# Retention scores in 64x64 array tiles, issued a tile ahead in one piece with the state product

## The chip, the core and the metric

The kernel runs on one core of a Trainium2 chip. The metric is the device time of one execution in microseconds (us), here the median of several executions. All five engines of the core (TensorE, called PE in the profile, with its weight loads PEld; VectorE, DVE; ScalarE, ACT; GpSimd, POOL; SyncE, SP) run their own instruction streams and meet at semaphores.

## The reference, cut to what matters

Three layers follow each other: a retention layer (a recurrent state with a decay for each head), a two-layer MLP with a layer norm, and a mixture of four attention experts of which two are chosen for each token. The change touches the first, and one matrix product of the third.

```python
# q, k, v: (B, H, S, D) = (2, 8, 768, 64)
for t in range(S):                                  # retention
    state = gamma * state + outer(k[t], v[t])
    y[t] = scale * q[t] @ state
x = y as (B, S, 512)
xn = layer_norm(x) * g_ln
x = x + relu(xn @ w_ch1) @ w_ch2                    # 512 -> 2048 -> 512
for e in range(4):                                  # attention experts, head dim 64
    a = softmax(causal(q_e @ k_e.T / 8))
    out += gate_e * (a @ v_e) @ wo[e]
```

## The kernel before

**Retention.** The sequence is cut into chunks of 128 tokens; with two batches that makes 12 tiles, which run in the order (chunk 0, batch 0), (chunk 0, batch 1), (chunk 1, batch 0) and so on. Each tile holds all 8 heads as 4 pairs. For each tile two arrays are loaded by DMA, `kq` (k and q with the head dimension on the partitions, 512 KB, four buffers) and `vk` (v and k with the tokens on the partitions, 512 KB, three buffers), and for each chunk a table `tabY` of 256 KB. `r_tile(i)` then plans:

- POOL scales v by the decay (`vs`, L425).
- `scores` on PE (L435): k transposed times q for each head. The contraction runs over the 64 dimensions of a head, so the two heads of a pair lie in the two row halves of the array (64 rows by 128 columns); 8 products, each of which the trace shows as 2 MATMULs with a weight load of its own.
- DVE multiplies the scores by the causal mask (`am`, L441, two of them).
- `inter` (L454, not for chunk 0): the state of the chunk before times q, in 64 by 64 array tiles, into two PSUM banks `y`.
- `intra` (L463): scaled values times masked scores, added into `y`, in array tiles of 128 rows by 64 columns.
- `upd` (L470, not for the last chunk): the state update, in 128 by 64 tiles too; ACT copies the state out (`sn`, L475), which the `inter` of the same batch's next chunk reads.
- DVE multiplies `y` by `tabY` into `xT` (L479), PE transposes it (L486, full array), DVE, POOL and ACT make the layer norm, PE transposes back (L486 again), ACT and POOL split the result into a high and a low part (`x`) for the MLP.

**PSUM.** It has 8 banks. The state takes one; scores, `y`, both transposes, the scratch of the weight splits and the MLP's sums share the other seven, taken and given back bank by bank.

**The planner.** Nothing is issued in the order of the program text. Every step becomes a `Node` with an engine, a cost in us, what it reads and writes, the buffers it takes, and a priority (`prio`, the order of planning, shifted by `P.bias`). `Plan.issue` plays the kernel through with these costs: whenever an engine is free, it takes the waiting step with the lowest priority number whose inputs are ready and whose buffers fit, all of them at once. The order found is the order in which each engine's instructions are written, DMAs included: they all go out through SP, one queue, and an SP instruction that waits for its buffer holds up those behind it.

**MLP and attention.** The MLP's weights are split into high and low parts as they come (L523 to L548), its products are L592, L611 and L672; for some weight blocks it uses sums of tokens (`x_sums`, POOL, L634 to L641). MLP steps of the first tokens are planned into the retention stage where PE would be idle. In attention `a_turn` (L905) transposes the probabilities and `a_value` (L924) multiplies them by the values, two experts side by side in array tiles of 128 by 64; L948 is the output projection.

Of the kernel before, what the change touches and what calls it, by code (L numbers as in the profile page):

```python
# [28 lines left out]
OP = mybir.AluOpType  # L29
# [7 lines left out]
C = 128  # L37
# [8 lines left out]
NPC = 4  # L46
LATE = 150
ALONE = 4
SEVEN = (2, 3, 4, 5, 6, 7)
NEG = -1000000000.0  # L50
LIMIT = float(np.array(0x0FEFFFFF, np.uint32).view(np.float32))
# [21 lines left out]


class Node:
    __slots__ = ("eng", "fn", "deps", "bufs", "prio", "lat", "end", "left", "succ", "ready")


class Plan:
# [5 lines left out]
        self.readers = {}  # L85
        self.bias = 0

    def add(self, eng, fn, r=(), w=(), lat=0.12, hold=()):
        n = Node()
        n.eng = eng  # L90
# [24 lines left out]
        self.nodes.append(n)  # L115

    def issue(self):
# [29 lines left out]
                    waiting[e].append(n)  # L147
        todo = len(self.nodes)
        order = []
        t = 0.0  # L150
        while todo:
            moved = True
            while moved:
                moved = False
                for e in free:
                    if free[e] > t:
                        continue
                    for n in sorted(waiting[e], key=lambda n: n.prio):
                        if n.ready > t:
                            continue  # L160
                        got = []
# [51 lines left out]
def retention_channel_mlp_mixture_attention(ctx: ExitStack, tc: tile.TileContext, a):  # L213
# [101 lines left out]
    def new(n):  # L315
        return Buf(PL[n], n)

    def PE(c, fn, r=(), w=(), hold=()):
        P.add({"T": c}, lambda e: fn(), r, w, lat=0.2, hold=hold)

    def ACT(c, fn, r=(), w=()):
        P.add({"A": c}, lambda e: fn(), r, w)
# [1 line left out]
    def DVE(c, fn, r=(), w=()):  # L324
        P.add({"V": c}, lambda e: fn(), r, w)
# [4 lines left out]
    def DMA(nbytes, fn, r=(), w=()):  # L330
        P.add({"D": nbytes / 320e3 + 0.05}, lambda e: fn(), r, w, lat=2.2)
# [27 lines left out]

    tiles = [(b, c) for c in range(NC) for b in range(B)]  # L360
    NTI = len(tiles)
    L = {}
    TY = {}

    def r4(ap):
        return ap.rearrange("p (a t) -> p a t", a=4)

    def load(i):
        b, c = tiles[i]
        kq, vk = new("kq"), new("vk")  # L370
        n = 2 if i == 0 else 1
        for y in range(n):
            h = slice(1024 // n * y, 1024 // n * (y + 1))
            DMA(512e3 / n, lambda h=h: sp.dma_start(f32(kq)[:, h], a["kq"][b, c][:, h]), w=[(kq, y)])
            if i == 0 and y == 0:
                DMA(24e3, lambda: sp.dma_start(tabV, a["tabV"]), w=["tabV"])
                DMA(64e3, lambda: sp.dma_start(caus, a["caus"]), w=["caus"])
        for y in range(n):
# [5 lines left out]
        L[i] = (kq, vk)  # L384

    DVE(0.2, lambda: dve.memset(negs, NEG), w=["negs"])
    IDLE = new("ps")
# [13 lines left out]
    DVE(0.1, lambda: dve.memset(half, -0.5), w=["half"])  # L401

# [11 lines left out]

    SN = {}

    def r_tile(i):
        b, c = tiles[i]
        j, cc = divmod(c, TPB)
        kq, vk = L[i]  # L420
        pair = lambda z, p: f32(kq)[:, p // 2 * 512 + z * 256 + p % 2 * C:p // 2 * 512 + z * 256 + (p % 2 + 1) * C]
# [6 lines left out]
        PA, AM = [new("ps") for _ in range(2)], [new("am") for _ in range(2)]  # L428
        ny = 2 if i == 0 else 1
        for y0 in range(ny):  # L430
            def scores(y0=y0):
                for p in range(4 // ny * y0, 4 // ny * (y0 + 1)):
                    for h in range(2):
                        hs = slice(64 * h, 64 * h + 64)
                        pe.matmul(f32(PA[h])[:, p * C:(p + 1) * C], lhsT=pair(0, p)[hs], rhs=pair(1, p)[hs],  # L435
                                  start=True, stop=True)
            PE(1.3 / ny, scores, r=[(kq, y0)] + (["spun"] if i == 0 else []), w=PA + (["scored"] if i == 0 else []), hold=AM)
            if i == 0 and y0:
                spin(2, 0.6, ["scored"], ["spun"])
        for h in range(2):  # L440
            DVE(0.69, lambda h=h: dve.tensor_tensor(r4(f32(AM[h])), r4(f32(PA[h])),  # L441
                                                    caus[:, None, :].to_broadcast([128, 4, C]), OP.mult),
                r=[PA[h], "caus"], w=[AM[h]])
# [3 lines left out]
        if c:  # L447
            def inter():
                for z in range(2):
                    for g in range(2):  # L450
                        for w in range(2):
                            p = 2 * z + g
                            ws = slice(64 * w, 64 * w + 64)
                            pe.matmul(place(g, w, z), lhsT=f32(st)[ws, p * D:(p + 1) * D], rhs=pair(1, p)[ws],  # L454
                                      start=(z == 0), stop=False, skip_group_check=True)
            PE(0.5, inter, r=[st, (kq, 0)], w=y)

        def intra():
            for w in range(2):
                for z in range(2):  # L460
                    for g in range(2):
                        p = 2 * z + g
                        pe.matmul(place(g, w, z), lhsT=h3(f32(vs))[:, 2 * p + w], rhs=r4(f32(AM[w]))[:, p],  # L463
                                  start=(c == 0 and z == 0), stop=True, skip_group_check=True)
        PE(1.0, intra, r=[vs] + AM + (y if c else []) + (["spun"] if i == 0 else []), w=y)
        if c < NC - 1:
            def upd():
                for p in range(NP):
                    for h in range(2):
                        pe.matmul(state(b)[64 * h:64 * h + 64, p * D:(p + 1) * D], lhsT=h3(k())[:, 2 * p + h],  # L470
                                  rhs=h3(f32(vs))[:, 2 * p + h], start=(i == 0 and p == 0), stop=False,
                                  skip_group_check=True)
# [438 lines left out]
    def a_value(b, g, p, PT, last, also=()):  # L911
        nj = 2 * g + 2
        avs, at = [new("psa") for _ in range(2 if last else 1)], new("at")
        for av, zs in zip(avs, ((0,), (1,)) if last else ((0, 1),)):
            for j0 in range(0, nj, 2):
                def mm(j0=j0, zs=zs, av=av):
                    for j in (j0, j0 + 1):
# [4 lines left out]
                        for x in range(2):  # L922
# [44 lines left out]

    pieces = [(f, i) for f in range(NFC) for i in ((2, 3, 0, 1) if f in SEVEN else range(NPC))]
    early = {0: (0, 1), 3: (2, 3), 7: (4, 5), 9: (6, 7)}
    for i in range(NTI):  # L970
        if i + 3 < NTI:
            load(i + 3)
        for n in early.get(i, ()):
            load_piece(*pieces[n])
        r_tile(i)
        for n in early.get(i, ()):
            P.bias += 40
            split_piece(*pieces[n])
            P.bias -= 40
# [129 lines left out]
```

## Time and profile before

| | |
|---|---|
| runs shown | 453.09, 452.96, 452.55 us; median 452.96 us |
| profiled execution, first to last instruction (span) | 450.3 us; no other time is recorded for it |
| PE busy | 439.8 us, 98% of the span |
| DVE, ACT, POOL busy | 328.0, 223.4, 209.4 us |
| granted TensorE clock | 1.000 over the span |
| retention on PE | 3.39 us to 67.9 us, from 39.4 us on with MLP steps among it |
| MLP, then attention | up to about 315 us, then to the end |

Busy times are from the profiled execution. A matmul's end is modelled and matmuls overlap, so the cost of a run of matmuls is best read as the distance from its start to the start of the next run on PE. [...]

### The profile page before, as it was taken

What the parts mean: (1) busy time and instruction counts of PE and PEld (TensorE: products, weight loads), DVE (VectorE), ACT (ScalarE), POOL (GpSimd) and SP (SyncE); (2) the same over time, 40 slices, a digit from 0 to 9 for tenths busy, and PEclk for the clock granted to TensorE, in tenths of its full rate; (3) what the DMA queues carried; (4) which work ended last, traced back from release to release, by engine and by line L of the source; (5) the groups of instructions that cost most, each with busy time, mean ns of one, the idle gap of its engine ahead of it and who ended that gap; (6) DMA issues with size and microseconds to landing.
All of it is one profiled execution on the core that took longest, in us unless ns stands there. A gap on an engine that the chain in (4) does not pass through costs nothing.

```text
span 450.3 us, 8468 instructions
## 1 busy us (share of the span) xinstructions
PE 439.8 (98%) x3198; PEld 415.5 (92%) x3198; DVE 328.0 (73%) x709; ACT 223.4 (50%) x467; POOL 209.4 (47%) x216
## 2 busy tenths in 40 slices
PE   8999999999999999999999999999999999998996
PEld 7778889999999999999999999999999987897875
DVE  2798786868659767877868565569657988878962
ACT  1476566263256335344354164245534756645852
POOL 1688768978989325226155064100401333224440
PEclk9999999999999999999999999999999999999999
DMA  7998923203103104114021002003230220101111
GB/s 263 366 347 325 314 81 108 95 24 118 47 1 140 48 1 134 55 48 140 1 89 53 1 1 93 2 0 95 70 72 20 66 71 33 49 1 47 49 49 47
DMA packets 15129, 40.11 MB, mean 89 GB/s; under 512 B 2288, under 2 KB 4976, under 8 KB 15088
## 3 DMA queue, kind: packets, MB, share of 16 engines
q1 hardware_dynamic: 15088, 39.57, 26.0%
q8 instruction: 25, 0.41, 0.4%
q14 instruction: 16, 0.13, 0.1%
HBM read 33.27 MB, written 3.15 MB: 81 GB/s over the span
## 4 chain that ended last, share of the span: by engine, by line
PE 86%; DVE 5%; DMA 3%; issue 2%; ACT 1%; POOL 1%; SPq 1%; DVEq 0%; ACTq 0%; POOLq 0%
PE ps L611 29%; PE ps L672 19%; PE ps L592 8%; PE ps L756 6%; PE ps L924 4%; PE ps L793 4%; PE ps L905 4%; PE ps L948 3%; DMA vk<-in_vk_dram 3%; PE ps L486 2%; PE ps L863 2%; PE ps L864 2%; PE ps L463 2%; PE ps L435 1%; DVE sm L871 1%
## 5 line engine op out<-in xcount | busy, mean ns | idle before, releaser
L611 PE MATMUL ps<-h,w 128*128 128x384 f32 x768 | 145.6, 335 | 0.7 <-DVE xT L615 0.4
L611 PEld LDWEIGHTS ps<-h,w 128*128 128x128 f32 x768 | 134.0, 188 | 1.4 <-DVE xT L615 0.7
L615 DVE TENSOR_TENSOR xT<-xT,ps 128x384 f32<-128x384 f32 x112 | 60.1, 549 | 36.9 <-PE ps L611 36.6
L885 POOL TENSOR_SCALAR pr<-pr,sm,gate 128x384 f32<-128x384 f32 (+5 forms) x48 | 34.9, 738 | 80.4 <-DVE ps L870 32.8
L548 POOL TENSOR_TENSOR w<-wy,w 128x512 fp32r<-128x512 f32 x26 | 33.7, 1301 | 44.2 <-PE ps L611 39.7
L672 PE MATMUL ps<-t,S 128*128 128x384 f32 x216 | 43.1, 334 | 0.0
L873 ACT ACTIVATE pr<-ps,sm 128x384 f32<-128x384 f32 (+5 forms) x48 | 30.3, 636 | 20.8 <-DVE sm L871 15.5
L679 ACT ACTIVATE u<-ps 128x384 f32<-128x384 f32 x36 | 17.6, 490 | 41.4 <-PE ps L672 35.7
L672 PEld LDWEIGHTS ps<-t,S 128*128 128x128 f32 x216 | 37.9, 188 | 0.1
L592 PE MATMUL ps<-x,w 128*128 128x384 f32 x192 | 34.8, 336 | 0.4 <-ACT wx L523 0.4
L523 ACT ACTIVATE wx<-raw 128x512 f32<-128x512 f32 x32 | 21.5, 672 | 27.5 <-DVE ps L527 19.7
L592 PEld LDWEIGHTS ps<-x,w 128*128 128x128 f32 x192 | 33.2, 188 | 0.8 <-ACT wx L523 0.6
L871 DVE TENSOR_REDUCE sm<-ps 128x1 f32<-128x384 f32 (+5 forms) x48 | 30.0, 624 | 2.9
L524 POOL TENSOR_SCALAR wx<-wx 128x512 f32<-128x512 f32 x32 | 20.3, 633 | 18.5 <-ACT wx L523 17.7
L687 ACT ACTIVATE h<-ps 128x384 fp32r<-128x384 f32 x36 | 17.6, 490 | 22.6 <-PE ps L611 14.4
L672 PE MATMUL ps<-x,w 128*128 128x384 f32 x144 | 28.8, 334 | 0.0
L672 PEld LDWEIGHTS ps<-x,w 128*128 128x128 f32 x144 | 25.3, 188 | 0.0
L905 PE MATMUL ps<-ident,pr 128*128 128x128 f32 x168 | 22.5, 275 | 2.0 <-DVE at L935 1.2
L547 ACT ACTIVATE w<-wy 128x512 fp32r<-128x512 f32 x26 | 16.3, 627 | 16.4 <-PE ps L611 16.1
L525 DVE TENSOR_SCALAR ps<-wx 128x512 uint32<-128x512 uint32 x32 | 22.0, 686 | 2.2 <-POOL wx L524 1.8
L529 DVE SCALAR_TENSOR_TENSOR wy<-raw,ps 128x512 uint32<-128x512 uint32 x32 | 21.8, 682 | 1.9 <-POOL w L548 1.3
L527 DVE SCALAR_TENSOR_TENSOR ps<-wx,ps 128x512 uint32<-128x512 uint32 x32 | 22.3, 696 | 1.1
(123 smaller groups left out, 877.3 us busy)
## 6 DMA issues: line engine op xcount, KB each, us to landing
raw<-in_w_dram SPq DMA_DIRECT2D x32, 512.0 KB, 3.5
kq<-in_kq_dram SPq DMA_DIRECT2D x11, 512.0 KB, 5.5
vk<-in_vk_dram SPq DMA_DIRECT2D x11, 512.0 KB, 5.1
qk<-qk SPq DMA_DIRECT2D x32, 96.0 KB, 2.1
out_dram<-ob SPq DMA_DIRECT2D x11, 256.0 KB, 2.0
tabY<-in_tabY_dram SPq DMA_DIRECT2D x6, 256.0 KB, 5.2
vraw<-in_wv_dram SPq DMA_DIRECT2D x1, 520.0 KB, 3.6
kq<-in_kq_dram SPq DMA_DIRECT2D x2, 256.0 KB, 2.9
```

The lines of the kernel that those rows point to most:

```text
L525: DVE(0.62, lambda: dve.tensor_scalar(u32(z), u32(x), 4, 1, op0=OP.logical_shift_left, op1=OP.logical_shift_right), r=[x], w=[z])
L527: DVE(0.7, lambda: dve.scalar_tensor_tensor(u32(z), u32(x), 0x80000000, u32(z), op0=OP.bitwise_and, op1=OP.bitwise_or), r=[x, z], w=[z])
L548: POOL(1.34, lambda: pool.tensor_tensor(f32r(l), f32(y), f32(h), OP.subtract), r=[y, h], w=[l])
L592: pe.matmul(f32(pa, TB), lhsT=wt, rhs=blk(f32r(xt[b][j]))[:, k], start=(n == 0), stop=(n == 11))
L611: pe.matmul(f32(pa, TB), lhsT=wt, rhs=t, start=(n == 0), stop=(n == 5))
L615: DVE(0.55, lambda: dve.tensor_tensor(blk(f32(xt))[:, k], blk(f32(xt))[:, k], f32(pa, TB), OP.add), r=[pa] + [(xt, cc, w) for cc in range( ...
L672: pe.matmul(f32(pa, TB), lhsT=wt, rhs=t, start=(first and n == 0), stop=(n == 5), skip_group_check=True)
L756: pe.matmul(f32(pa, TB), lhsT=mw(n, lo, k, p * 128, (p + 1) * 128), rhs=blk(f32r(xt))[:, k], start=(i == 0), stop=(i == 11))
L871: dve.tensor_reduce(f32(sm)[:, z:z + 1], halves(f32(s), 512), axis=mybir.AxisListType.XY, op=OP.max, negate=True)
L873: ACT(act_c(nk) + .18, lambda s=s, pr=pr, z=z: act.activation(halves(f32(pr), wide), halves(f32(s), 512), AF.Exp, bias=f32(sm)[:, z:z + 1] ...
L885: POOL(0.28 + nk * 0.95e-3, lambda pr=pr, z=z, e=e: pool.tensor_scalar(f32(pr, nk), f32(pr, nk), f32(sm)[:, 6 + z:7 + z], GT[b, j][:, cc, ...
L905: pe.transpose(f32(pa)[:, i * C:(i + 1) * C], f32(PRS[z][x])[:, j * C:(j + 1) * C], ident)
```

## The change

Four things are edited; the computation stays the same.

1. The scores of tile i+1 are planned inside `r_tile(i)`, and in one PE step with the state product `inter` of tile i (`quarters`). Each 128-column weight block of the scores is cut in two, so that they run in 64 by 64 array tiles: 16 products for each tile instead of 8. The first tile's scores stand alone (`r_first`). The step takes the two `y` banks and the two score banks (`PAS`) together, and holds the two mask buffers (`AMS`).
2. `upd` and `intra` become one PE step (`columns`), the update first, except in the first tile and in the last chunk.
3. `load` is cut into `load_kq` and `load_vk`, and `kq` is planned one tile further ahead than `vk`.
4. Each PE step has a form (whole, quarters, columns). In the planner a step of another form than the last one is sorted 25 places later (`STAY`), and costs 0.16 us more (`SWITCH`). `a_value` is of the form columns, and its planned cost falls from 0.97 and 0.76 to 0.85 and 0.64.

```diff
+STAY = 25
+SWITCH = 0.16
...
-                    for n in sorted(waiting[e], key=lambda n: n.prio):
+                    for n in sorted(waiting[e], key=lambda n: n.prio + STAY * (e == "T" and n.form != form)):
...
                             cost = n.eng[e]
+                            if e == "T":
+                                cost += SWITCH * (n.form != form)
+                                form = n.form
...
-    load(0)
+    load_kq(0)
+    load_vk(0)
     DMA(64e3, lambda: sp.dma_start(ident, a["ident"]), w=["ident"])
-    load(1)
-    load(2)
+    load_kq(1)
+    load_vk(1)
+    load_kq(2)
+    load_kq(3)
+    load_vk(2)
...
+    def scores(i, ps):
+        for p in ps:
+            for m in range(2):
+                for h in range(2):
+                    hs, ms = slice(64 * h, 64 * h + 64), slice(64 * m, 64 * m + 64)
+                    pe.matmul(f32(PAS[i][h])[ms, p * C:(p + 1) * C], lhsT=pair(i, 0, p)[hs, ms], rhs=pair(i, 1, p)[hs],
+                              start=True, stop=True)
+
+    def masked(i):
+        for h in range(2):
+            DVE(0.69, lambda h=h: dve.tensor_tensor(r4(f32(AMS[i][h])), r4(f32(PAS[i][h])),
+                                                    caus[:, None, :].to_broadcast([128, 4, C]), OP.mult),
+                r=[PAS[i][h], "caus"], w=[AMS[i][h]])
...
-            PE(1.3 / ny, scores, r=[(kq, y0)] + (["spun"] if i == 0 else []), w=PA + (["scored"] if i == 0 else []), hold=AM)
...
-            PE(0.5, inter, r=[st, (kq, 0)], w=y)
...
+        if c or i + 1 < NTI:
+            def quarters():
+                if c:
+                    inter()
+                if i + 1 < NTI:
+                    scores(i + 1, range(4))
+            r, w, hold = [], [], []
+            if c:
+                r, w = [st, (KQ[i], 0)], list(y)
+            if i + 1 < NTI:
+                r, w, hold = r + [(KQ[i + 1], 0)], w + PAS[i + 1], AMS[i + 1]
+            PE(0.45 * bool(c) + 0.9 * (i + 1 < NTI), quarters, r=r, w=w, hold=hold, form="quarters")
+        if i + 1 < NTI:
+            masked(i + 1)
...
-        PE(1.0, intra, r=[vs] + AM + (y if c else []) + (["spun"] if i == 0 else []), w=y)
...
+        if c == NC - 1:
+            PE(0.86, intra, r=r1, w=w1, form="columns")
+        elif i == 0:
+            PE(0.86, intra, r=r1, w=w1, form="columns")
+            PE(0.45, upd, r=r2, w=w2, form="columns")
+        else:
+            def columns():
+                upd()
+                intra()
+            PE(1.31, columns, r=r1 + r2, w=w1 + w2, form="columns")
...
-            PE(0.65, upd, r=[(vk, 1), vs] + (["first"] if i == 1 else []), w=[(STATE, b)] + (["first"] if i == 0 else []))
...
-                PE((0.97 if j0 + 2 < nj else 0.76) * len(zs) / 2, mm,
+                PE((0.85 if j0 + 2 < nj else 0.64) * len(zs) / 2, mm, form="columns",
...
+    r_first()
     for i in range(NTI):
+        if i + 4 < NTI:
+            load_kq(i + 4)
         if i + 3 < NTI:
-            load(i + 3)
+            load_vk(i + 3)
```

## Rows read from the trace of the kernel before

**Rows 1.** The page: busy time of PE and DVE, busy tenths of PE and DMA.

```profile
PE 439.8 (98%) x3198; PEld 415.5 (92%) x3198; DVE 328.0 (73%) x709; ACT 223.4 (50%) x467; POOL 209.4 (47%) x216
...
PE   8999999999999999999999999999999999998996
...
DMA  7998923203103104114021002003230220101111
```

**Rows 2.** Windows: stretch, its length, busy us (count) by engine, clock, DMA share, GB/s.

```profile
12.50:20.00 7.50, 7.50 (x123) 6.27 (x124) 5.20 (x14) 2.78 (x5) 4.20 (x6) 1.00 0.96 359
20.00:26.80 6.80, 6.12 (x96) 4.77 (x94) 6.63 (x14) 6.11 (x11) 5.07 (x9) 1.00 0.94 342
...
32.00:38.00 6.00, 5.87 (x105) 5.09 (x105) 4.17 (x10) 4.33 (x8) 5.46 (x8) 1.00 0.98 370
```

**Rows 3.** Timeline of POOL: the value scaling of two tiles.

```profile
18.90 1.04 POOL L425 TENSOR_TENSOR vs<-vk,tabV 128x512 f32<-128x512 f32 x1 [0.39 <-DMA vk<-in_vk_dram]
...
25.74 1.04 POOL L425 TENSOR_TENSOR vs<-vk,tabV 128x512 f32<-128x512 f32 x1
```

**Rows 4.** Timeline of PE in retention: start us, us, engine, line, operation.

```profile
26.84 1.09 PE L463 MATMUL ps<-am,vs 128*64 128x128 f32 x16 [0.60 <-POOL vs L425]
27.76 0.64 PE L470 MATMUL ps<-vs,vk 128*64 128x64 f32 x16
28.32 1.16 PE L435 MATMUL ps<-kq 64*128 64x128 f32 x16
29.49 0.67 PE L454 MATMUL ps<-kq,sn 64*64 64x128 f32 x16
30.09 0.66 PE L486 MATMUL ps<-ident,xT 128*128 128x128 f32 x4
...
33.35 0.63 PE L470 MATMUL ps<-vs,vk 128*64 128x64 f32 x16
33.92 0.67 PE L454 MATMUL ps<-kq,sn 64*64 64x128 f32 x16
34.52 0.66 PE L486 MATMUL ps<-ident,xn 128*128 128x128 f32 x4
...
46.26 0.69 PE L470 MATMUL ps<-vs,vk 128*64 128x64 f32 x16
46.87 1.16 PE L435 MATMUL ps<-kq 64*128 64x128 f32 x16
47.97 1.09 PE L463 MATMUL ps<-am,vs 128*64 128x128 f32 x16
48.99 0.66 PE L486 MATMUL ps<-ident,xn 128*128 128x128 f32 x4
```

**Rows 5.** Timeline of PE: the first MLP step in retention.

```profile
39.37 2.32 PE L592 MATMUL ps<-x,w 128*128 128x384 f32 x12 [0.38 <-ACT wx L523]
```

**Rows 6.** Timeline of weight loads and DVE, 26 to 34 us.

```profile
29.01 0.76 DVE L479 TENSOR_TENSOR xT<-ps,tabY 128x256 f32<-128x256 f32 x2
29.49 0.43 PEld L454 LDWEIGHTS ps<-kq,sn 64*64 64x64 f32 x16 [0.20 <-DVE xT L479]
...
30.09 0.42 PEld L486 LDWEIGHTS ps<-ident,xT 128*128 128x128 f32 x4 [0.17 <-issue]
```

**Rows 7.** Groups by line on PE: busy us, mean ns | idle before.

```profile
L435 PE MATMUL ps<-kq 64*128 64x128 f32 x192 | 15.2, 299 | 1.1 <-DMA kq<-in_kq_dram 1.0
...
L454 PE MATMUL ps<-kq,sn 64*64 64x128 f32 x160 | 6.8, 282 | 0.0
```

**Rows 8.** Waits of SP's queue, 0 to 70 us: total, times, longest.

```profile
SPq L374 <- PE ps L454: 13.7, 6, 3.5
```

**Rows 9.** Timeline of PE: one run of attention's value products.

```profile
425.88 3.25 PE L924 MATMUL ps<-ptn,vv 128*64 128x256 f32 x32
```

**Rows 10.** Timeline of POOL: the last token sums of the MLP.

```profile
142.59 3.65 POOL L641 TENSOR_TENSOR t<-t,t 128x768 fp32r<-128x768 f32 x2
```

**Rows 11.** Timeline of PE: a product that reads token sums.

```profile
146.52 1.20 PE L672 MATMUL ps<-t,S 128*128 128x384 f32 x6
```

More of the change, by code (lines that the diff above doesn't have):

```diff
@@ L75 @@
 class Node:
-    __slots__ = ("eng", "fn", "deps", "bufs", "prio", "lat", "end", "left", "succ", "ready")
+    __slots__ = ("eng", "fn", "deps", "bufs", "prio", "lat", "end", "left", "succ", "ready", "form")
 class Plan:
@@ L86, in __init__, with add @@
         self.bias = 0
-    def add(self, eng, fn, r=(), w=(), lat=0.12, hold=()):
+    def add(self, eng, fn, r=(), w=(), lat=0.12, hold=(), form="whole"):
         n = Node()
+        n.form = form
         n.eng = eng
@@ L149, in issue @@
         order = []
+        form = "whole"
         t = 0.0
@@ L316, in new, with PE @@
         return Buf(PL[n], n)
-    def PE(c, fn, r=(), w=(), hold=()):
-        P.add({"T": c}, lambda e: fn(), r, w, lat=0.2, hold=hold)
+    def PE(c, fn, r=(), w=(), hold=(), form="whole"):
+        P.add({"T": c}, lambda e: fn(), r, w, lat=0.2, hold=hold, form=form)
     def ACT(c, fn, r=(), w=()):
@@ L361, in retention_channel_mlp_mixture_attention, with load_kq @@
     NTI = len(tiles)
-    L = {}
-    TY = {}
+    KQ, VK, TY, PAS, AMS = {}, {}, {}, {}, {}
     def r4(ap):
         return ap.rearrange("p (a t) -> p a t", a=4)
-    def load(i):
+    def load_kq(i):
         b, c = tiles[i]
-        kq, vk = new("kq"), new("vk")
+        kq = new("kq")
         n = 2 if i == 0 else 1
@@ L377, in load, with load_vk @@
                 DMA(64e3, lambda: sp.dma_start(caus, a["caus"]), w=["caus"])
+        KQ[i] = kq
+    def load_vk(i):
+        b, c = tiles[i]
+        vk = new("vk")
+        n = 2 if i == 0 else 1
         for y in range(n):
@@ L383, in load @@
             DMA(256e3, lambda: sp.dma_start(f32(ty), a["tabY"][c]), w=[ty])
-        L[i] = (kq, vk)
+        VK[i] = vk
     DVE(0.2, lambda: dve.memset(negs, NEG), w=["negs"])
@@ L415, in retention_channel_mlp_mixture_attention, with pair, r_first @@
     SN = {}
+    def pair(i, z, p):
+        return f32(KQ[i])[:, p // 2 * 512 + z * 256 + p % 2 * C:p // 2 * 512 + z * 256 + (p % 2 + 1) * C]
+    def scores(i, ps):
[10 more added lines that the diff above has]
+                r=[PAS[i][h], "caus"], w=[AMS[i][h]])
+    def r_first():
+        PAS[0], AMS[0] = [new("ps") for _ in range(2)], [new("am") for _ in range(2)]
+        for y0 in range(2):
+            PE(0.45, lambda y0=y0: scores(0, range(2 * y0, 2 * y0 + 2)), r=[(KQ[0], y0), "spun"], w=PAS[0] + ["scored"], hold=AMS[0],
+               form="quarters")
+        spin(2, 0.6, ["scored"], ["spun"])
+        masked(0)
     def r_tile(i):
@@ L419, in r_tile @@
         j, cc = divmod(c, TPB)
-        kq, vk = L[i]
-        pair = lambda z, p: f32(kq)[:, p // 2 * 512 + z * 256 + p % 2 * C:p // 2 * 512 + z * 256 + (p % 2 + 1) * C]
+        vk = VK[i]
         v, k = lambda: f32(vk)[:, :512], lambda: f32(vk)[:, 512:]
@@ L427, in r_tile @@
              r=[(vk, 0), "tabV"], w=[vs])
[L428 to L436, printed above, removed]
-            PE(1.3 / ny, scores, r=[(kq, y0)] + (["spun"] if i == 0 else []), w=PA + (["scored"] if i == 0 else []), hold=AM)
[L438 to L443, printed above, removed]
         st = SN.get(b)
@@ L446, in r_tile, with inter @@
         place = lambda g, w, z: f32(y[w])[64 * g:64 * g + 64, z * C:(z + 1) * C]
[L447 to L455, printed above, removed]
-            PE(0.5, inter, r=[st, (kq, 0)], w=y)
+        def inter():
+            for z in range(2):
+                for g in range(2):
+                    for w in range(2):
+                        p = 2 * z + g
+                        ws = slice(64 * w, 64 * w + 64)
+                        pe.matmul(place(g, w, z), lhsT=f32(st)[ws, p * D:(p + 1) * D], rhs=pair(i, 1, p)[ws],
+                                  start=(z == 0), stop=False, skip_group_check=True)
+        if i + 1 < NTI:
+            PAS[i + 1], AMS[i + 1] = [new("ps") for _ in range(2)], [new("am") for _ in range(2)]
+        if c or i + 1 < NTI:
[10 more added lines that the diff above has]
+            PE(0.45 * bool(c) + 0.9 * (i + 1 < NTI), quarters, r=r, w=w, hold=hold, form="quarters")
+        if i + 1 < NTI:
+            masked(i + 1)
         def intra():
@@ L462, in intra, with upd @@
                         p = 2 * z + g
-                        pe.matmul(place(g, w, z), lhsT=h3(f32(vs))[:, 2 * p + w], rhs=r4(f32(AM[w]))[:, p],
+                        pe.matmul(place(g, w, z), lhsT=h3(f32(vs))[:, 2 * p + w], rhs=r4(f32(AMS[i][w]))[:, p],
                                   start=(c == 0 and z == 0), stop=True, skip_group_check=True)
-        PE(1.0, intra, r=[vs] + AM + (y if c else []) + (["spun"] if i == 0 else []), w=y)
-        if c < NC - 1:
[L467 to L472, printed above, removed]
-            PE(0.65, upd, r=[(vk, 1), vs] + (["first"] if i == 1 else []), w=[(STATE, b)] + (["first"] if i == 0 else []))
+        def upd():
+            for p in range(NP):
+                for h in range(2):
+                    pe.matmul(state(b)[64 * h:64 * h + 64, p * D:(p + 1) * D], lhsT=h3(k())[:, 2 * p + h],
+                              rhs=h3(f32(vs))[:, 2 * p + h], start=(i == 0 and p == 0), stop=False,
+                              skip_group_check=True)
+        r1, w1 = [vs] + AMS[i] + (y if c else []) + (["spun"] if i == 0 else []), list(y)
+        r2, w2 = [(vk, 1), vs] + (["first"] if i == 1 else []), [(STATE, b)] + (["first"] if i == 0 else [])
+        if c == NC - 1:
[8 more added lines that the diff above has]
+            PE(1.31, columns, r=r1 + r2, w=w1 + w2, form="columns")
+        if c < NC - 1:
             sn = SN[b] = SNB[b][c % 2]
```

## The prediction

> **What bounds the kernel now.** I read the page first. PE is busy 98% of the span, no other engine above 73%, and PE's busy tenths read 9 in nearly every slice after the first. But the line of the DMA shows 7 to 9 tenths in the first five slices, 56 us, and little after them [rows 1]. So the kernel is bound by PE, with one stage, retention, in which the loads run at the same time at their limit. The change lies almost wholly in that stage, so I cut it into windows [rows 2]: from 12.5 to 20 us the DMA share is 0.96 at 359 GB/s, from 32 to 38 us 0.98 at 370 GB/s, with PE at 5.87 of 6.00 us there. Two limits lie close to each other. What is saved on PE is worth its full size only where PE ends last; where PE waits for `vk`, it is worth nothing.
>
> Then I looked for where the one passes to the other. POOL's value scaling at 18.90 us started when a `vk` had landed, 0.39 us late [rows 3], and at 26.84 us PE waited 0.60 us for the scaling that began at 25.74 us [rows 3, 4]. From there to the end of retention I found one wait of 0.38 us, in front of an MLP step that the planner had put into retention [rows 5]; from there on PE has such filler work. So I call the time up to 26.84 us bound by loads, and all after it bound by PE.
>
> **What one piece costs.** I read costs from start to start in the timeline [rows 4]. The scores take 1.17 us before `inter` (28.32 to 29.49) and 1.10 us before `intra` (46.87 to 47.97). `inter` takes 0.60 us, at both places. `intra` takes 0.92 us when `upd` follows in the same tile shape (26.84 to 27.76), and 1.02 us when the full array follows (47.97 to 48.99). `upd` takes 0.56 us, or 0.61 us at 46.26. Where the shape changes, the weight load stands idle 0.17 us for nothing but the issue, and the 16 loads of `inter` take 0.43 us [rows 6]; 0.43 and 0.17 are the 0.60 us of `inter`. So a change of shape costs 0.17 us, and 16 instructions in 64 by 64 tiles cost 0.43 us.
>
> **The change, part by part.**
>
> *Scores in quarters, in one step with `inter`.* The 192 MATMULs of the scores become 384 [rows 7], 32 for each tile, half as wide in the weights. No row shows scores in quarters; the nearest is `inter`, the same shape with the same 128 moving columns. By it 32 instructions cost 0.86 us, and with `inter` and one change of shape the step costs 0.86 + 0.43 + 0.17 = 1.46 us, against 1.70 to 1.77 us before. That saves 0.24 to 0.31 us; I take 0.27. Nine steps hold both (tiles 2 to 10): 2.4 us. Two hold scores alone, 1.03 us against 1.10 to 1.17: 0.2 us together. From the other side: if the denser stream of instructions cannot be fed, it costs, and that is a rival below.
>
> *`columns`.* Together `upd` and `intra` cost 0.92 + 0.56 = 1.48 us, apart 1.02 + 0.61 = 1.63 us. Of the ten tiles with an update the timeline has them together in five already. Five times 0.15 is 0.75 us. The state copy on ACT still starts after `upd`, which now goes first in its step. Both now wait for scaled values and masked scores; the masks are planned a tile earlier, so the values come last, as before.
>
> Together that is 3.4 us less of PE.
>
> *`kq` a tile ahead of `vk`.* In SP's queue one more `kq` of 512 KB stands before each `vk`. At 359 GB/s that is 1.46 us, by which each `vk` lands later in the stretch that the DMA limits. A `kq` is also loaded into the buffer of tile i where it was i-1 before, so its DMA waits for a later PE step; SP already spends 13.7 us waiting for `inter` at that line [rows 8]. Behind the waiting instruction stand the next `vk`, `tabY` and weight pieces. With three tiles between the load and its use, and the DMA at its limit anyway, I price that wait at nothing; if the lead is too short, it costs what a transfer is late.
>
> *Where this counts.* After 26.84 us there are six of the nine double steps and two of the five parted pairs: 6 x 0.27 + 2 x 0.15 = 1.9 us. One set of scores, 1.1 us, moves from after the wait for values to before it, where PE has time. That makes 3.0 us. If the `vk` that ends that wait lands a full transfer later, 1.5 us are left. If it is no later (the scaling at 25.74 us shows no wait for a DMA, it came behind other POOL work), the whole saving of 3.4 us may come out. One row speaks for the delay and one against [rows 3]; I take 2.3 us, about midway.
>
> *The forms in the planner.* A step that changes the shape goes back 25 places. This can put transposes together; one change less for each of twelve tiles is at most 12 x 0.17 = 2.0 us. I count nothing, since the planner's own trials cannot be read from the trace. In attention the value products already run as long runs, 32 MATMULs in one at 425.88 us [rows 9]; a change of shape more or less for three of them is 0.5 us in either direction, and I count nothing. The cover is PE work that stands ready; without it a value product put back delays the output projection by its wait.
>
> [...] `inter` runs at 0.43 us for 16, 27 ns each [rows 6]. [...]
>
> **The sum.** The profiled span is 450.3 us, the median of the runs 452.96 us; the 2.7 us around the span do not change. 450.3 - 2.3 = 448.0 us of span, so **450.7 us**. With the bounds (1.5 to 3.4 us, and 0.5 us from attention) the likeliest case reaches from 449.1 to 452.0 us. 0.2% of this kernel, 0.9 us, is about what a measurement can tell from no change.
>
> **Rivals.**
>
> *Given back in the MLP (no change).* POOL makes the last token sums from 142.59 to 146.24 us, and PE begins a product on such sums at 146.52 us [rows 10, 11]. If POOL's chain does not move forward with retention, PE is early there and waits: the 2.3 us are gone, 453.0 us. For it: the margin is 0.3 us. Against: the sums are made from retention's output, which comes earlier too, and POOL is busy only 47% of the span [rows 1]. 12 in 100. The loads can do the same if both the earlier `vk` and the later `kq` hurt; 5 in 100 more.
>
> *Four banks at once (slower).* The new step takes two `y` banks and two score banks together; seven are shared. The last tile's `y` comes free only when DVE has multiplied it, 0.76 us for both halves [rows 6], and DVE is busy 6.63 of 6.80 us around there [rows 2]. If PE has nothing else at that moment, it stands 0.76 us at each of nine steps, 6.8 us: 457.5 us. The change loses from 0.26 us on for each step (2.3 over 9). For it: steps that take more at once fit later. Against: a transpose takes 0.59 us (0.42 and 0.17, [rows 6]) and covers most of it, and from 39 us on MLP steps do. 10 in 100.
>
> *The stream cannot be fed (slower).* A tile has 72 MATMULs now and 88 then. The densest window has 105 in 6.00 us, 57 ns each [rows 2]. If that is as fast as instructions come, a tile goes from 4.1 to 5.0 us, and eleven tiles cost 10 us: 463 us. For it: no row shows 48 MATMULs in a row at 27 ns. Against: `upd` and `inter` after 33.35 us are 32 in 1.17 us, 37 ns each with two changes of shape [rows 4]. 5 in 100. [...]
>
> **How the numbers follow.** The forecast has 68 in 100, the two ways to no change 17, the two to a slower kernel 15. Faster 0.68, same 0.17, slower 0.15. The range takes in the planner's 2.0 us below (449.1 less 2.0 is 447.1; I say 447.3), and above it the cases of no change and the lower part of the bank rival (a hole of 0.42 us costs 3.8, less 2.3 is 1.5 us: 454.5). Outside lie the fed stream, most of the bank rival, and the last of the gain, some 17 in 100.
>
> **What would show it.** Right, if a `quarters` step of 48 MATMULs reads 1.4 to 1.5 us from start to start and `columns` 1.5 us, if the last back transpose of retention and the first products on token sums both come some 2 us earlier, and PE has no more idle time after 27 us than now. Wrong, if POOL waits longer for `vk` in the first 30 us; if PE waits for DVE's `y` before `quarters`; if the step takes well over 1.5 us; or if the gain at 70 us is gone at 150.

## The result, and the profile after

The median of four runs after is 458.3 us (457.76 to 458.87), beside 453.02 us (452.55 to 453.79) of the kernel before on the same chip. The ratio is 1.0115, with a 95% interval from 1.0102 to 1.0128: by it the change costs 5.2 us (the ratio is one of means; the medians lie 5.3 us apart). 450.7 us was forecast, and the range ended at 454.5.

The page after, the lines that answer to [rows 1]: PE has 192 MATMULs more and is busy 1.1 us less, in a span that is 5.4 us longer (455.7 us; the profiled execution itself took 457.76 us).

```profile
PE 438.7 (96%) x3390; PEld 415.8 (91%) x3390; DVE 325.8 (71%) x709; ACT 224.5 (49%) x468; POOL 209.0 (46%) x215
...
PE   7979998999999999999999999999999999999996
...
DMA  7989832202202203204112002002220221101111
```

So PE didn't get more to do, it stood. Where, the waits of PE over the first 100 us show (total us, times, the longest). Before, no wait in retention was over 0.7 us (the 1.0 us at L404 stands in front of dummy products at the very start, in both kernels).

```profile
PE ps L538 <- ACT xn L554: 2.6, 3, 1.6
PE ps L478 <- DVE wy L581: 2.2, 1, 2.2
PE ps L404 <- DVE half L417: 1.0, 1, 1.0
PE ps L441 <- DMA kq<-in_kq_dram: 1.0, 2, 0.6
PE ps L509 <- DMA vk<-in_vk_dram: 0.8, 1, 0.8
PE ps L538 <- DVE xT L531: 0.6, 1, 0.6
PE ps L644 <- POOL x L561: 0.5, 1, 0.5
```

The timeline of PE, with the rows that answer to [rows 4, 5], and behind it four rows of before that no group above has. L478 is `inter`, L441 the scores; they are one step now. L509 is `upd`, L503 `intra`, L538 a transpose, L644 and L663 MLP products.

```profile
28.23 1.04 PE L503 MATMUL ps<-am,vs 128*64 128x128 f32 x16
31.49 0.67 PE L478 MATMUL ps<-kq,sn 64*64 64x128 f32 x16 [2.21 <-DVE wy L581]
31.98 1.05 PE L441 MATMUL ps<-kq 64*64 64x128 f32 x32
32.96 0.66 PE L538 MATMUL ps<-ident,xT 128*128 128x128 f32 x4
...
34.35 0.69 PE L509 MATMUL ps<-vs,vk 128*64 128x64 f32 x16
34.86 1.05 PE L503 MATMUL ps<-am,vs 128*64 128x128 f32 x16
35.84 0.67 PE L478 MATMUL ps<-kq,sn 64*64 64x128 f32 x16
...
40.72 2.18 PE L644 MATMUL ps<-x,w 128*128 128x384 f32 x11 [0.46 <-POOL x L561]
...
70.28 1.09 PE L503 MATMUL ps<-am,vs 128*64 128x128 f32 x16
71.95 0.77 PE L538 MATMUL ps<-ident,xT 128*128 128x128 f32 x4 [0.58 <-DVE xT L531]
74.30 1.11 PE L538 MATMUL ps<-ident,xn 128*128 128x128 f32 x4 [1.58 <-ACT xn L554]
75.08 3.42 PE L663 MATMUL ps<-h,w 128*128 128x384 f32 x12
78.34 0.60 PE L538 MATMUL ps<-ident,xn 128*128 128x128 f32 x4
...
127.69 1.20 PE L724 MATMUL ps<-t,S 128*128 128x384 f32 x6
...
149.10 1.33 PE L663 MATMUL ps<-h,w 128*128 128x384 f32 x6 [1.48 <-DVE wy L581]
```

```profile
62.21 1.09 PE L463 MATMUL ps<-am,vs 128*64 128x128 f32 x16
...
74.02 0.60 PE L486 MATMUL ps<-ident,xn 128*128 128x128 f32 x4
...
124.05 1.20 PE L672 MATMUL ps<-t,S 128*128 128x384 f32 x6
...
143.27 3.42 PE L611 MATMUL ps<-h,w 128*128 128x384 f32 x18 [0.33 <-DVE wy L529]
```

Three things stand here. First, the new pieces cost what was forecast: `quarters` 31.49 to 32.96, 1.47 us; `columns` 34.35 to 35.84, 1.49 us. Second, at 31.49 us the joint step had waited 2.21 us for L581, the DVE step that ends the split of a weight block and gives back the PSUM bank of its scratch. `inter` has nothing to do with that weight block; but the step needs four banks at once, and one of the four was still held there. Third, the last values come at 70.28 us, before at 62.21 us. Ahead of them PE now has 72 MLP MATMULs, before 30; the 42 more are some 7.6 us, at 2.16 us for 12. That work isn't lost, but it is missing at the end of retention: no MLP product stands between 70.28 and 75.08 us. PE waits 1.58 us for the layer norm of the last tile but one, and the 12 MATMULs after 75.08 us take 3.26 us to the next row on PE, where 12 in 128x384 took 2.16 us before (from 39.37 us, [rows 5], to the next row on PE at 41.53 us). Retention's last back transposes come at 78.34 us, before at 74.02 us. (The 67.9 us in the table ahead of the prediction is the end of the last tile's first transposes; retention ends with these.)

The windows of that stretch and those that answer to [rows 2] (columns as there):

```profile
12.50:20.00 7.50, 7.50 (x172) 6.46 (x164) 6.62 (x15) 2.66 (x5) 2.55 (x5) 1.00 0.98 353
20.00:26.80 6.80, 5.82 (x118) 4.84 (x120) 5.14 (x12) 4.36 (x8) 5.80 (x9) 1.00 1.02 374
32.00:38.00 6.00, 5.86 (x134) 4.94 (x127) 3.75 (x9) 4.43 (x8) 5.09 (x6) 1.00 0.99 376
70.00:75.00 5.00, 2.84 (x28) 2.06 (x25) 4.40 (x13) 3.03 (x6) 3.01 (x5) 0.90 0.10 17
75.00:80.00 5.00, 5.00 (x25) 4.90 (x25) 3.11 (x6) 3.92 (x7) 4.76 (x6) 0.76 0.55 193
```

The stream can be fed: 134 MATMULs in 6.00 us, 45 ns each, where before had 57 ns. And the granted clock, 1.00 of full speed here before, falls to 0.90 from 70 to 75 us, where PE stood for 2.16 of the 5.00 us, and to 0.76 from 75 to 80 us.

**The balance.** The sums of the windows over the first 125 us, before and after:

```profile
sum 125.00, PE 120.89 PEld 111.07 DVE 92.60 ACT 62.24 POOL 95.47; mean PE 12.09 PEld 11.11 DVE 9.26 ACT 6.22 POOL 9.55
```

```profile
sum 125.00, PE 116.27 PEld 107.48 DVE 88.66 ACT 61.88 POOL 92.05; mean PE 11.63 PEld 10.75 DVE 8.87 ACT 6.19 POOL 9.21
```

The same product, the first on token sums, starts at 124.05 us before and at 127.69 us after, 3.6 us later. PE stands 4.1 us before (120.89 busy) and 8.7 us after (116.27): 4.6 us more. Nearly all of it lies behind 27 us: from there to 125 us PE stands 0.9 us before and 5.0 us after. The clock took 2.84 x 0.10 + 5.00 x 0.24 = 1.5 us, an estimate from the busy times and the clocks of the last two windows above. That makes 6.1; only 3.6 arrived, so the new pieces do save about 2.5 us of PE work, an estimate from this balance; the idle time and the clock cost more than that. Later 1.1 us are added where PE waits at 149.10 us for a weight split (1.48 us; the like wait before is 0.33 us at 143.27), and 0.6 us in attention.

### The profile page after: what moved, and what is told of

It reads as the page before. It is cut to its first block, busy times and chain, and to the rows that moved or that the text cites. A ratio compares the mean times of both kernels' runs of the same rounds, so it can differ in the third digit from the quotient of the medians.

```text
span 455.7 us, 8847 instructions
## 1 busy us (share of the span) xinstructions
PE 438.7 (96%) x3390; PEld 415.8 (91%) x3390; DVE 325.8 (71%) x709; ACT 224.5 (49%) x468; POOL 209.0 (46%) x215
## 4 chain that ended last, share of the span: by engine, by line
PE 83%; DVE 9%; ACT 3%; issue 2%; DMA 1%; POOL 1%; SPq 0%; DVEq 0%; POOLq 0%
PE ps L663 29%; PE ps L724 19%; PE ps L644 7%; PE ps L808 5%; PE ps L845 4%; PE ps L976 3%; PE ps L1000 3%; PE ps L957 3%; DVE sm L923 2%; PE ps L441 2%; PE ps L503 2%; PE ps L538 2%; PE ps L915 2%; PE ps L916 1%; DMA vk<-in_vk_dram 1%
## 5 line engine op out<-in xcount | busy, mean ns | idle before, releaser
L663 PE MATMUL ps<-h,w 128*128 128x384 f32 x768 | 147.4, 337 | 1.5 <-DVE wy L581 1.5
L663 PEld LDWEIGHTS ps<-h,w 128*128 128x128 f32 x768 | 135.1, 189 | 2.2 <-DVE wy L581 1.8
L644 PE MATMUL ps<-x,w 128*128 128x384 f32 x192 | 35.3, 337 | 0.5 <-POOL x L561 0.5
L644 PEld LDWEIGHTS ps<-x,w 128*128 128x128 f32 x192 | 33.2, 188 | 1.2 <-POOL x L561 0.7
L577 DVE TENSOR_SCALAR ps<-wx 128x512 uint32<-128x512 uint32 x32 | 22.0, 689 | 3.2 <-POOL wx L576 3.1
L581 DVE SCALAR_TENSOR_TENSOR wy<-raw,ps 128x512 uint32<-128x512 uint32 x32 | 21.9, 683 | 2.8 <-POOL w L600 2.2
L579 DVE SCALAR_TENSOR_TENSOR ps<-wx,ps 128x512 uint32<-128x512 uint32 x32 | 22.2, 694 | 1.0
```

The source lines that it names most:

```text
L577: DVE(0.62, lambda: dve.tensor_scalar(u32(z), u32(x), 4, 1, op0=OP.logical_shift_left, op1=OP.logical_shift_right), r=[x], w=[z])
L579: DVE(0.7, lambda: dve.scalar_tensor_tensor(u32(z), u32(x), 0x80000000, u32(z), op0=OP.bitwise_and, op1=OP.bitwise_or), r=[x, z], w=[z])
L644: pe.matmul(f32(pa, TB), lhsT=wt, rhs=blk(f32r(xt[b][j]))[:, k], start=(n == 0), stop=(n == 11))
L663: pe.matmul(f32(pa, TB), lhsT=wt, rhs=t, start=(n == 0), stop=(n == 5))
```

## The experiments

Ratios are to the kernel before, run on the same chip, with 95% intervals. Line numbers in the profile of an edited kernel are shifted by a few.

**Parts alone, on the kernel before.** First the quarter scores without anything else: planned costs and issue order are those of before.

```diff
-                    for h in range(2):
-                        hs = slice(64 * h, 64 * h + 64)
-                        pe.matmul(f32(PA[h])[:, p * C:(p + 1) * C], lhsT=pair(0, p)[hs], rhs=pair(1, p)[hs],
...
+                    for m in range(2):
+                        for h in range(2):
+                            hs, ms = slice(64 * h, 64 * h + 64), slice(64 * m, 64 * m + 64)
+                            pe.matmul(f32(PA[h])[ms, p * C:(p + 1) * C], lhsT=pair(0, p)[hs, ms], rhs=pair(1, p)[hs],
...
```

> The kernel before, with nothing changed but the scores, which run in 64x64 array tiles; planned costs and so the order on every engine stay those of before. Theory P (PE time in retention counts in full after 27 us): a set of scores goes from 1.10-1.17 us to 1.03 us, seven sets after 27 us, so 0.5 to 1.0 us faster. Theory C (retention ends by a chain through loads, VectorE and GpSimd, and PE time saved there turns into idle time): no change, within 0.3 us.

0.9981 [0.9969, 0.9992], 0.9 us faster. From its timeline of PE, a tile's scores (L436) and the next row:

```profile
32.22 1.10 PE L436 MATMUL ps<-kq 64*64 64x128 f32 x32
33.25 0.66 PE L487 MATMUL ps<-ident,xn 128*128 128x128 f32 x4
```

1.03 us beside 1.10 us before, or 1.17 us where `inter` followed: the seven sets after 27 us are worth 0.5 to 1.0 us at that. In the profiled execution the values start 1.47 us behind those of before at 33.90 us and 0.81 us behind at 63.02 us, so 0.66 us were won in between. With the order kept, the array tiles pay.

Then a test of whether PE's time in retention counts at all: half of the state product and half of the update left out, order kept.

```diff
-                for z in range(2):                      # inter
+                for z in range(1):
-                for p in range(NP):                     # upd
+                for p in range(NP if c == 0 else NP // 2):
```

> The kernel before in its own order, with half of the state product (four of eight products in each tile) and half of the state update (four of eight, from the second chunk on) left out, so that retention has 0.43 us less PE work in each tile and the output is not the retention's. Theory P: seven half state products and six half updates lie after 27 us, 13 times 0.21, so 2.7 us faster. Theory C: less than 0.8 us faster, and PE's idle time in retention grows by some 2 us.

0.994 [0.9925, 0.9954], 2.7 us less. PE's time counts, so the first step of the prediction stands.

The load order alone (`load_kq` one tile ahead of `load_vk`, item 3 of the change):

> The kernel before with one part of the change alone: kq loaded one tile further ahead than vk. Theory D (the later vk costs): 1 to 2 us slower, with GpSimd's value scaling later by about 1.5 us for tiles 2 to 4. Theory B (the slowdown comes from the PSUM banks of the joint step): within 0.5 us of before.

1.0014 [1.0005, 1.0023], 0.6 us slower. And `columns` alone (item 2):

```diff
-        PE(1.0, intra, ...)
-            PE(0.65, upd, ...)
+                PE(1.5, lambda: (upd(), intra()), r=[vs, (vk, 1)] + AM + ..., w=y + [(STATE, b)])
```

> The kernel before with the state update and the values joined into one PE step, as the change does, and nothing else. My sum of the prediction: five pairs at 0.15 us, 0.3 to 0.8 us faster. Theory G (a coarser step fits later into the order, so the planner lets the retention chain slip, and PE idles at its end): 1 us or more slower, with the values of the last tile, at 62.2 us before, at 65 us or later.

1.0051 [1.0037, 1.0065], 2.3 us slower, where the prediction had booked 0.75 us saved. In its list of waits PE waits 2.2 us for `xn`, in four places; the list of before has no such entry.

**Parts undone, on the kernel after.** The joint step cut in two again, in the same array tiles and a tile ahead:

```diff
-            PE(0.45 * bool(c) + 0.9 * (i + 1 < NTI), quarters, r=r, w=w, hold=hold, form="quarters")
+            if c:
+                PE(0.45, inter, r=[st, (KQ[i], 0)], w=list(y), form="quarters")
+            if i + 1 < NTI:
+                PE(0.9, lambda: scores(i + 1, range(4)), r=[(KQ[i + 1], 0)], w=PAS[i + 1], hold=AMS[i + 1], ...)
```

> The kernel after, with the joint step cut into its two halves, the state product (two banks) and the next tile's scores (two banks), each planned on its own. Theory B (the step that takes four banks at once is late, and MLP steps take its place on PE): faster than the kernel after by 2 us or more, the wait of 2.2 us before the state product at 31.5 us gone, and the state product of the eighth tile, at 45.8 us in the kernel after, before 42 us. Theory D or the forms being the cause: within 1 us of the kernel after, at about 1.01 of before.

1.005 [1.0033, 1.0067]: 2.9 us of the 5.2 come back, and the wait of 2.2 us for the bank is gone.

No preference for a form (`STAY = 0` instead of 25):

> The kernel after with STAY at 0, so that a change of form still costs 0.16 us in the plan but no longer puts a step back by 25 places. Theory F (the forms delay retention's steps and attention's value products): faster than after by 1 us or more, and attention, from the first key projection to the end, back from 135.8 to 135.2 us. Theory B: retention does not move, attention wins its 0.6 us, so at most 0.7 us faster than after.

1.0056 [1.0031, 1.008]. `kq` no further ahead than `vk` (three tiles, as before):

> The kernel after with kq loaded three tiles ahead beside its vk, as before, and no longer four. Theory D (the later vk costs): faster than after by about 0.6 us, which is what this part cost alone in the kernel before (1.0014). Rival: the scores of the next tile need kq early, so slower than after by 1 us or more.

1.007 [1.0047, 1.0092]. All of these undone in one kernel, and `columns` parted too (STAY 4; quarter scores still a tile ahead):

> The kernel after with both joint steps cut again, kq three tiles ahead and STAY at 4: what is left of the change is the scores in quarters, planned a tile ahead, and the price of a change of form. Theory G (joint steps, load order and STAY carry the loss): within 1 us of before, 0.998 to 1.002. Rival: scores a tile ahead hold two banks and two mask buffers for longer and carry the loss themselves: 1.005 or more.

0.9997 [0.9984, 1.0009]. Each of the three alone gives back 2 to 3 us (7.6 in all); the four together give back 5.3: the parts don't add up. (The gap of 2.3 us is hardly more than the intervals, taken together, leave open: some 2.1 us.) That was the first sign that each edit does something else beside its own work.

**The wait for the bank.** Two experiments on its mechanism. If later MLP steps slip past the waiting joint step and take the banks it needs, a planner that lets no later step take a bank meanwhile should help:

```diff
...
+                        if first is not None and n.prio > first.prio and any(b.at is None and b.kind == "ps" for b in n.bufs):
+                            continue
...
```

> The kernel after with one rule more in the planner: while a joint step of scores and state product is ready and finds no banks, no step behind it may take a bank. Theory B1 (MLP steps that slip in ahead of the joint step cause the loss): the state product of the eighth tile comes back from 45.8 us to 42 us or earlier, and the kernel is 2 us or more faster than after. Theory G: the joint step waits on PE instead, with idle time in place of MLP steps, and the kernel is within 1 us of after.

1.0092 [1.0063, 1.012]: no clear gain, and PE now waits three times, 5.0 us, for such banks. The theory found no support here; since this planner too found another order, the run doesn't rule it out. Then the scratch of the first eight weight splits in SBUF instead of a bank:

```diff
-        DVE(0.62, lambda: dve.tensor_scalar(u32(z), u32(x), 4, 1, op0=OP.logical_shift_left, ...
+        DVE(0.62, lambda: dve.tensor_scalar(scratch(), u32(x), 4, 1, op0=OP.logical_shift_left, ...
...
```

> The kernel after in its own order, with one thing changed: the scratch of the first eight weight splits lies in SBUF instead of the PSUM bank that the planner gave it, so that no PE step has to wait for a split to give a bank back. Theory B (banks): the wait of 2.2 us before the state product at 31.5 us goes away; since the order is fixed, one part of the 5.3 us comes back, 1 to 2.5 us, unless the loads or VectorE hold the same step up by nearly as long. If the wait was for VectorE's other work: no change, and the wait stays under another name.

1.0241 [1.0223, 1.0259], far slower. The joint step that had waited now starts at 28.82 us with no wait (only its scores then wait, 0.61 us, for DVE's masks), so it was that bank. But some of the split's operations took twice as long, 1.44 and 1.41 us for 0.68 and 0.70 us (last section), and what the wait was worth the run can't say.

**The clock.** Six products whose result is overwritten (`negs` times `negs`, 12 MATMULs) stand before the back transposes of the eleventh tile, so that PE works while it waits for the layer norm of that tile:

```diff
+            if i == NTI - 2:
+                for _ in range(6):
+                    pe.matmul(f32(t2)[:, :C], lhsT=negs, rhs=negs, start=True, stop=True)
...
```

> The kernel after in its own order, with six dummy products of 128 columns on PE in front of the back transposes of the eleventh tile, where PE stood idle for 1.6 us; they wait for nothing and their result is overwritten. Theory K (the idle time at the end of retention lowers PE's clock, and that costs time by itself): the granted clock stays at 1.00 from 70 to 80 us and the kernel is 1.2 to 1.6 us faster than after, at about 1.0085 of before. If the clock costs nothing: no change.

1.0085 [1.0065, 1.0106]. The window that after had at 0.76:

```profile
75.00:80.00 5.00, 4.71 (x29) 4.44 (x30) 3.99 (x10) 4.62 (x9) 4.46 (x7) 1.00 0.51 179
```

The clock stays up there, at 1.00, and the 12 MATMULs that took 3.26 us take 2.21 us (75.95 us to the next row at 78.16 us). By the ratios alone that is worth some 1.3 us, the size of the sum above, but the two intervals just overlap, and over the profiled span the mean clock is 0.996 in both kernels: in this one it fell from 30 to 40 us, to 0.83. The size is not settled.

**The order itself.** Apart from the quarter scores, the work left out, the scratch and the dummy products, every edit so far also made the planner find another order. So the last question was what an order is worth with the instructions left as they are: only planned costs are changed, on the kernel before first. As the trace shows them, all four:

```diff
-            PE(1.3 / ny, scores, ...
+            PE(1.12 / ny, scores, ...
...
-            PE(0.5, inter, ...
+            PE(0.6, inter, ...
...
-        PE(1.0, intra, ...
+        PE(0.97, intra, ...
...
-            PE(0.65, upd, ...
+            PE(0.57, upd, ...
```

> The kernel before with the same instructions; only four costs in the plan are set to what the trace shows (scores 1.12 us, state product 0.60, values 0.97, state update 0.57, where the plan had 1.3, 0.5, 1.0 and 0.65). Theory R (the order found by the planner is worth some us by itself, and the order of before is a good one among many, so that any new plan of retention loses): 1 to 3 us slower, 1.002 to 1.007 of before. Theory G (the loss comes from the coarser steps, the load order and STAY as such): within 0.8 us of before, or faster for the truer costs.

1.0101 [1.0077, 1.0125]. PE's instructions are those of before, and nearly the whole loss of the change is there. (Two additions of weight sums, 128x256 each, went from POOL to DVE, since the planner also chooses the engine of a few such steps; in each plan below one or two such steps change engine too.) Its longest waits, both in retention, with L486 the transposes and L435 the scores:

```profile
PE ps L486 <- ACT xn L502: 3.3, 4, 1.3
PE ps L435 <- DMA kq<-in_kq_dram: 2.7, 3, 1.5
```

One cost alone, `upd` 0.55 instead of 0.65:

> The kernel before with the same instructions and one cost of the plan changed: the state update at 0.55 us instead of 0.65. Theory R: 0.5 to 2 us slower, with more idle time of PE in retention. Theory G: within 0.8 us of before.

1.0037 [1.0026, 1.0047]. `inter` 0.60 instead of 0.50:

> The kernel before with the same instructions and one cost of the plan changed: the state product at 0.60 us instead of 0.50. Theory R: 0 to 1 us slower. Theory G: within 0.8 us of before. The three runs of plans together: under theory R most of them are slower than before by more than the measurement's interval, and none is faster.

1.0031 [1.0014, 1.0049].

Then the same on the kernel after. `columns` planned at 1.35 instead of 1.31 us:

> The kernel after, with the planned cost of the joint update-and-values step 1.35 instead of 1.31 us; the instructions are the same, the planner finds another order. If the joint steps as such cost the time, it stays where after is, 1.009 to 1.014 of before. If the order decides, it can lie anywhere between 1.00 and 1.02.

1.0067 [1.0053, 1.0081]. Lower costs throughout (`inter` 0.40, scores 0.80, `columns` 1.19):

> The kernel after, with lower planned costs: state product 0.40 for 0.45, scores 0.80 for 0.90, update with values 1.19 for 1.31 us. Same instructions, another order. Joint steps as such: 1.009 to 1.014 of before. Order decides: this order may well be the better one, 0.995 to 1.007; a time at or under before would show that nothing in the changed steps needs to lose.

1.0042 [1.0026, 1.0058]. `columns` at 1.14 us:

> The kernel after, with the planned cost of the joint update-and-values step 1.14 instead of 1.31 us; same instructions, another order. Joint steps as such: 1.009 to 1.014 of before. Order decides: anywhere from 0.995 to 1.015, and apart from the other two plans by more than their intervals.

1.0066 [1.0043, 1.009]. So the same steps of PE, in four orders, take 1.0042 to 1.0115. The bank wait of the joint step is in all three (longest 1.2, 2.5 and 2.5 us, in the order of the runs above), the wait at the end of retention for a layer norm in none at its full size (longest wait for `xn` 0.9, 1.1 and 0.4 us). The clock falls in two of them, to 0.83 from 30 to 40 us in the second and in the third (there also to 0.90 and 0.93 in the first 20 us), and stays at 1.00 in the first; in the kernel of the lower costs the 0.83 stand behind a stretch in which PE stood for 2.7 of 10 us:

```profile
20.00:30.00 10.00, 7.30 (x148) 5.83 (x136) 8.74 (x18) 6.90 (x13) 7.87 (x11) 1.00 0.91 325
30.00:40.00 10.00, 9.55 (x176) 8.19 (x176) 6.58 (x16) 6.28 (x12) 7.67 (x11) 0.83 0.88 311
```

**What can be kept.** The order of before in retention, quarter scores, and forms for attention's value products alone (`STAY = 8`):

> The kernel before, its retention order unchanged, with the scores in 64x64 array tiles, and the form of the value products in attention with SWITCH 0.16 and STAY 8. The scores alone gave 0.9981 of before; attention, 135.2 us from the first key projection to the end, may give 0 to 0.5 us. Expected 0.997 to 0.998 of before. If STAY of 8 does in attention what 25 did, 0.6 us are lost: 0.9995.

0.9982 [0.9971, 0.9993]: faster than both kernels, and no better than the quarter scores alone, so the forms bring nothing that can be seen.

## Why the prediction was wrong

**Right: what a piece costs.** 1.46 and 1.48 us were forecast, 1.47 and 1.49 us came. A change of shape at 0.17 us and 16 products in 0.43 us carry over to a piece that no row had shown. 48 MATMULs in 1.47 us are 31 ns each, so the rival of the stream that can't be fed is out.

**Right: PE's time in retention counts** (the run with work left out), and some 2.5 of the 3.4 us of PE work were saved.

**Not settled: the load order.** About half of the full transfer of 1.46 us was booked; alone the new order cost 0.6 us. That is near, but this run has another issue order too, so the 0.6 us isn't the price of a later `vk` alone. The sign that the prediction named for it, longer waits of POOL for `vk`, didn't come: 10.3 us before and 10.2 us after, over the first 76 us.

**Wrong: "The forms in the planner" as a term of zero, "since the planner's own trials cannot be read from the trace".** This is the step that failed, and it failed for more than the forms. The sum went through before's timeline tile by tile ("six of the nine double steps") and took shorter pieces in the same places, with the same filler work beside them ("all after it bound by PE"). But the planner re-orders everything when a cost, a form or a grouping changes, and the order is worth more than the edit: 0.3 to 1.0% for the same instructions of before, 0.7% between the best and the worst order of the changed ones. What came in place of the zero is idle time: behind 27 us, up to 125 us, PE stands 5.0 us instead of 0.9, though "no more idle time after 27 us than now" was the prediction's own sign of being right. `columns` is the plainest case: booked as 0.75 us saved, with no cost for the coarser step, it lost 2.3 us alone. That nothing could be read was a reason for a wide bound to the slow side, not for a zero; I had given it 2.0 us to the fast side and 0.5 us to the slow one.

**Half right: "Four banks at once".** The rival had the sign and a real wait. But it priced nine waits of 0.76 us for the multiplication of `y`, and there came one of 2.21 us, for a weight split's scratch that it didn't think of. I had gone through the readers of the four buffers and not through the other users of the same seven banks. The rival "Given back in the MLP" was right that a wait would come there (149.10 us, 1.48 us, shortly before the product it named), but not why: DVE's weight split released it and not POOL's sums, and PE came there late and not early.

**What is shown and what stays open.** Shown: other orders of the same PE instructions lose 0.3 to 1.0%, and the changed ones lie anywhere from 0.4 to 1.15% above before. Open is how much the joint steps lose as such. The three other plans of before's steps have a mean of 1.0056, the four of the changed steps 1.0072; the difference of 0.7 us is far less than the spread among either, but the changed ones have some 2.5 us less PE work and should lie lower. The kernel with all joints parted came to 0.9997, on one plan. So the joints probably cost something, by the banks they wait for; four orders don't settle it. Why before's order is a good one, better than that from the costs its own trace shows, wasn't found either: the waits name what is late in the others (`kq`, `xn`, a bank), not one cause. One sign is common to them: the last values start at 62.21 us before, at 63.9 to 66.0 us in five of the six new plans, and at 70.03 and 70.28 us in the two slowest (`b_plan_a` and the kernel after); ahead of them stand 30 MLP MATMULs before, 36 to 48 in the new plans, 72 after. It looks as if the slower orders spent filler work early that the end of retention then lacks, but no run changes that alone, so it isn't shown to be the cause.

## What to carry to other kernels

Where a greedy planner writes the order, make an edit first with the plan held still (the same planned costs, steps and priorities), and then the new plan by itself, with the instructions held still; only so are the edit's saving and the order's loss told apart. Run a few plans with slightly different costs before you believe in any of them: here 0.04 us in one planned cost moved the kernel by half a per cent. And a step that takes several buffers at once waits for the last of them, so go through all other users of the pool before you join two steps.

## What the hardware showed that was not expected

When the weight split's scratch went from PSUM to SBUF, some of DVE's operations on it took twice as long. The same two operations, on DVE's timeline, first after, then with the scratch in SBUF:

```profile
25.04 0.68 DVE L577 TENSOR_SCALAR ps<-wx 128x512 uint32<-128x512 uint32 x1
25.76 0.70 DVE L579 SCALAR_TENSOR_TENSOR ps<-wx,ps 128x512 uint32<-128x512 uint32 x1
```

```profile
24.64 1.44 DVE L585 TENSOR_SCALAR zs<-wx 128x512 uint32<-128x512 uint32 x1
26.12 1.41 DVE L587 SCALAR_TENSOR_TENSOR zs<-wx,zs 128x512 uint32<-128x512 uint32 x1
...
31.81 0.69 DVE L587 SCALAR_TENSOR_TENSOR zs<-wx,zs 128x512 uint32<-128x512 uint32 x1
```

L587 took 0.69 us later, at 31.81 us, when POOL ran only operations of 128x1. POOL was stretched as well. Its value scaling takes 1.04 to 1.05 us in the kernel after (at 21.60, 26.15 and 31.76 us); with the scratch in SBUF:

```profile
21.20 1.05 POOL L465 TENSOR_TENSOR vs<-vk,tabV 128x512 f32<-128x512 f32 x1
...
25.76 1.22 POOL L465 TENSOR_TENSOR vs<-vk,tabV 128x512 f32<-128x512 f32 x1
...
32.59 1.53 POOL L465 TENSOR_TENSOR vs<-vk,tabV 128x512 f32<-128x512 f32 x1
```

So L587 took 1.41 us where POOL's scaling ran beside it (25.76 to 26.98 us). Work on POOL alone doesn't do it: with the operand in PSUM, in the kernel after, L579 took 0.70 us at 25.76 us, beside a POOL operation up to 26.19 us (L561, 128x512) and the scaling from 26.15 us on. The split's first operation (L585, `zs<-wx`) was stretched as well: 1.44 us at 24.64 us, beside L561 on POOL from 24.53 to 25.80 us, where the kernel after has 0.68 us at 25.04 us (L577) beside the same POOL operation, 24.92 to 26.19 us. What holds the two engines up when the scratch lies in SBUF, no run shows. I moved a buffer to free a bank and got slower operations on it instead.
